# Batch 0's q rows projected from float16 pairs that the load queue transposes

## The chip, the core and the metric

The kernel runs on one core of a Trainium2 chip. A core has five engines with an instruction stream each: TensorE (PE: matrix products and transposes into PSUM; PEld is its weight load), VectorE (DVE), ScalarE (ACT), GpSimd (POOL) and SyncE (SP), on which nearly all DMA transfers of this kernel are issued. The metric is the device time of one execution in microseconds, as the median of several runs. The numbers of the profile come from one profiled execution.

## The reference

Attention with random features over 4 batches and 8 heads (576 rows of 64), then two gated layers. All in float32:

```python
def phi(x):                              # x is q or k, times 64 ** -0.25
    proj = np.einsum('bhsd,md->bhsm', x, omega)        # 128 features
    h = proj - np.sum(x * x, axis=-1, keepdims=True) / 2.0
    h = h - np.max(h, axis=-1, keepdims=True)
    return np.exp(h) / np.sqrt(m)
q_p, k_p = phi(q_s), phi(k_s)
kv  = np.einsum('bhsm,bhsd->bhmd', k_p, v)
num = np.einsum('bhsm,bhmd->bhsd', q_p, kv)
den = np.einsum('bhsm,bhm->bhs', q_p, np.sum(k_p, axis=2))[..., None] + 1e-06
x = (num / den)                          # -> 2304 tokens x 512
h = x @ w_in                             # 512 x 2048
x = (h / (1 + np.exp(-1.702 * h))) @ w_out
out = ((x @ w_a) * (x @ w_b)) @ w_o2     # 512 x 1536, twice; 1536 x 512
```

## The kernel before

**Stages.** Batch 0's attention runs alone, in the first 50 us or so. Then the first gated layer of batch b (`ffn1`) runs interleaved with the attention of batch b+1, token tile by token tile (four of 512 tokens, and one of 256 with the rest rows). The second gated layer (`ffn2`) is last. A product that has to keep float32's accuracy is made of float16 pairs: each operand is a scaled high part (ScalarE) and the remainder, its low part (VectorE), and TensorE makes three products of them.

**Attention, per head pair.** Two heads are worked on together, four head pairs per batch; k of a pair in `kphase32`, q in `qphase`. Both call `features`, which transposes the raw rows (128 partitions of `raw`), projects them on `omega`, takes the maximum of each row (`mx`, line 813), makes the exponent's bias from it and the row's squares `sq` (`mh` and `nb`, line 819) and takes exponentials on ScalarE (`e`, line 779). For batch 0, rows go through TensorE in float32: four transposes against `ident` (line 719), an evacuation with a scale into `xt` (line 665 on VectorE for the names in `EVX`, line 666 on ScalarE for the others), and 16 products that use half of the array's rows each (line 730). For batches 1 to 3 the rows become a float16 pair (`x16`, printed `x_k` or `x_q`; high part at line 734 on ScalarE, low part at line 735 on VectorE), SyncE transposes that by DMA into `xt` (line 740), and TensorE makes two full-array products per block of 128 rows (lines 746 and 747). A head pair's 512 main rows are handled so in batch 0; the remaining 64 rows of all heads go together as `restk` and `restq` (lines 674 to 707). The sum of keys times v is line 874 (and 872 for the rest rows); q's side has transposes of `e` (line 898) and products with it (line 905).

**First gated layer.** `ph` are the three products of h (lines 993 to 995), `th` and `gl` VectorE's part of the gate (lines 1005 and 1015), `gh` ScalarE's, and `y` the three products of the output (1028 to 1030). Line 1029 is the one that uses the low part `gl`.

**Weights.** They come as 64-bit floats, by chunks of 1 MB on SyncE (`wraw`, line 479, two buffers). VectorE turns a chunk into float32 by bit operations (`wf`, lines 493, 533 and 541), ScalarE writes the high part (line 551), VectorE the low part (line 500). Chunks alternate between `w_in` and `w_out`.

**What sets the order.** Each engine's stream is an order written out: the table `ORDER` holds a permutation of the program's instructions for each engine, and an engine executes in that order, so one instruction that waits holds all behind it. SyncE's stream is the load queue too. Its loads are raw rows (line 626; small remainders at 631), rest rows (639), v (`vt` at 650, `vm` at 652) and weights (479). Buffers: the tag A (`x16`, `restk`, `restq`) has two, B (`xt`) two, raw k three, raw q four.

The lines that decide where batch 0 differs:

```python
if nm[1] == "0":                       # batch 0: TensorE transposes
    ...
groups, pairs = (GROUPS_F, PAIRS_F) if nm[1] == "0" else (GROUPS, PAIRS)
```

Of the kernel before, what the change touches and what calls it, by code (L numbers as in the profile page):

```python
# [38 lines left out]
    "uQv0/rnF++cG758fve9twhm+372raBnvOj7uAtwzcu6pOPe8HAtiNSyzNbZQVuku0blrH/eJx1jBe+O7/ifc4z78Xfpz4+Dc4Djh"
    "dveRbzycGxznRsVJy38f+S7kuSt57jKeu47nLuQpB3lvd9fv3JN/7pk/fvl4Zvced2XOXZYzYtQ97u1uaJwbC+cGw2mPItzuMd9A"  # L40
    "OjeSznjQ+5/jP+/j3XA4dw3PXcRzo+LcsDg3Ls4NjHNX9TxdEvfGTze+D3WX79x1PDcwzl35c0PjvFw793Yvt7uPfNf83HU7d+GO"
    "VbvLd+6KxV3yuEsed8nDkt+IOm93u79DfLxdjXdl7tLGjZu4MRMPj3J/euMjjivyPpS1vIscrmSX8l6r9743bsJl7fp2cbuq79JG"
    "eLx7uxsbcYMmXMN3BeOuYHgZcP2ni//e7q5q3FWNu6rx9uX+4D79uE8/7tOPt5eP+1Ce1l2oSC8zHuX+Z/nPe+Mbu3HDJ24gxT2n"
    "cc9p3AWIuxRxVyHuKsRdhbznJe+JzXti8+F799Xk4eXL65YjvUcwHuU+8g2paK949+Fv/MV44buPfIMmxvXhbvfGTy+F98Y3cuJG"
    "TtzIiRs5cSMnbuTEjZy4ERF3aePtHvcw7oLmXdC8C5r3PKfzfGMo71rm8YP7jO4R5HhVvD+9R5D3CPIuY97DyHsY+fRCfJ/5XdW8"
    "pzPv6cx7OvOuQr796z7U03293N7v3RDIu7R5FzTv+qYXda/8XvLveuQ9demV+sZa3ljL45jvTcJR3fuG+96Humc3317HvZDfm3hp"
    "vyc77/Vb90TUw7/88vvI/gp4+U+//N7jRljeCMtyu3v099rP9qfj/h24q18P/7qPclehji+v++UewT3IugdZ9yAr/Cm5d7unru6p"
    "q3s2yjO/L0F5X6Dqnvu6577uua972uue9nr6G3Tv68ncE1tPf5PuQ/lL1f51H+UeafkLdc9B+Xu1f7z8Nl/u870veHlfDvPGaY44"
# [1571 lines left out]
```

## Time and profile before

| | us |
|---|---|
| runs, median of three | 862.88 |
| runs, lowest and highest | 862.5 and 863.72 |
| profiled execution, its own time | 863.73 |
| span of the profiled execution | 861.9 |
| granted TensorE clock, mean | 0.999 of full speed |

The span is the time from the first to the last recorded instruction; the execution takes 1.8 us more. The stages table gives, for a stretch, the time each engine was busy in it and the number of its instructions. The chain of waits goes back from the end: at each moment it names the piece of work that everything behind it stood on. In a timeline an instruction's own time is its record; two records on one engine may overlap by a few hundredths, so what an instruction takes of its engine is better read from one start to the next. Idle time before an instruction stands in brackets, with what ended it.

### The profile page before, as it was taken

The page shows a single profiled execution, that of the slowest core. Times are in us where ns is not written, and L with a number is a line of the kernel's source. Part 1 is how long each engine was busy: PE and PEld are TensorE (multiplying, and loading weights), DVE is VectorE, ACT ScalarE, POOL GpSimd, SP SyncE. Part 2 cuts the span into 40 slices and gives each one's busy share as a digit, 9 for nine tenths or more (in the row PEclk, how much of TensorE's full clock was granted, in tenths as well). Part 3 has the DMA queues.
Part 4 walks back from the last instruction along what each step waited for, and adds up shares of the span by engine and source line. Part 5 has one row for each costly group of instructions (what it writes and reads, how often), then busy time and mean ns, then how long its engine had stood idle before and what let it go on. Part 6 is the DMA issues. An engine that isn't in the chain of part 4 may idle for free.

```text
span 861.9 us, 17314 instructions
## 1 busy us (share of the span) xinstructions
PE 851.8 (99%) x7064; PEld 616.8 (72%) x7064; DVE 677.1 (79%) x1224; ACT 456.6 (53%) x1087; POOL 1.5 (0%) x11
## 2 busy tenths in 40 slices
PE   9999999999999999999999999999999999999997
PEld 7865555455555555444468888889888899888896
DVE  5999999999999977799111489969999758456766
ACT  6997886787767766654232555344543313123221
POOL 0000000000000000000000000000000000000000
PEclk9999999999999999999999999999999999999999
DMA  9977699937674235665110215412522202123312
GB/s 247 245 203 209 177 225 241 222 79 180 146 166 128 77 69 96 140 215 183 49 50 2 83 78 184 159 44 87 183 87 86 44 11 106 68 100 122 89 42 74
DMA packets 138735, 107.71 MB, mean 125 GB/s; under 512 B 107168, under 2 KB 120480, under 8 KB 136608
## 3 DMA queue, kind: packets, MB, share of 16 engines
q1 hardware_dynamic: 138080, 106.05, 45.4%
q8 instruction: 55, 0.90, 0.4%
q10 hardware_dynamic: 576, 0.56, 0.2%
q14 instruction: 24, 0.20, 0.1%
HBM read 71.07 MB, written 17.69 MB: 103 GB/s over the span
## 4 chain that ended last, share of the span: by engine, by line
PE 83%; DVE 9%; DMA 4%; ACT 3%; issue 1%; ACTq 0%; SPq 0%; DVEq 0%
PE ph L993 5%; PE ph L994 5%; PE ph L995 5%; PE y L1029 5%; PE y L1028 5%; PE y L1030 5%; PE paA L1152 3%; PE paA L1153 3%; PE paA L1154 3%; PE pbA L1152 3%; PE pbA L1154 3%; PE pbA L1153 3%; PE oA L1248 3%; PE oA L1250 3%; PE oA L1249 3%; DMA eqT_q<-e_q 2%
## 5 line engine op out<-in xcount | busy, mean ns | idle before, releaser
L1029 PE MATMUL y<-gl,w_out 128*128 128x512 f16 (+1 forms) x320 | 113.6, 358 | 0.3
L1030 PE MATMUL y<-gh,w_out 128*128 128x512 f16 (+1 forms) x320 | 113.3, 358 | 0.0
L1028 PE MATMUL y<-gh,w_out 128*128 128x512 f16 (+1 forms) x320 | 112.0, 358 | 0.0
L1015 DVE SCALAR_TENSOR_TENSOR gl<-th,gh 128x512 f16<-128x512 f32 (+1 forms) x80 | 50.5, 633 | 67.2 <-ACT gh L1014 67.0
L993 PE MATMUL ph<-xT,w_in 128*128 128x512 f16 x256 | 96.9, 379 | 0.6 <-DVE th L1005 0.6
L994 PE MATMUL ph<-xT,w_in 128*128 128x512 f16 x256 | 97.0, 379 | 0.0
L995 PE MATMUL ph<-xT,w_in 128*128 128x512 f16 x256 | 96.8, 379 | 0.0
L1153 PE MATMUL pbA<-forms,w_b 128*128 128x256 f16 (+1 forms) x240 | 61.1, 262 | 0.0
L1152 PE MATMUL pbA<-forms,w_b 128*128 128x256 f16 (+1 forms) x240 | 61.1, 262 | 0.0
L1154 PE MATMUL pbA<-forms,w_b 128*128 128x256 f16 (+1 forms) x240 | 61.0, 262 | 0.0
L1154 PE MATMUL paA<-forms,w_a 128*128 128x256 f16 (+1 forms) x240 | 61.0, 262 | 0.0
L1153 PE MATMUL paA<-forms,w_a 128*128 128x256 f16 (+1 forms) x240 | 61.0, 262 | 0.0
L1152 PE MATMUL paA<-forms,w_a 128*128 128x256 f16 (+1 forms) x240 | 61.0, 262 | 0.0
L1248 PE MATMUL oA<-w_o,ab 128*128 128x256 f16 x216 | 58.9, 273 | 0.3 <-DVE o L1256 0.3
L1250 PE MATMUL oA<-w_o,ab 128*128 128x256 f16 x216 | 58.9, 273 | 0.0
L1249 PE MATMUL oA<-w_o,ab 128*128 128x256 f16 x216 | 58.9, 273 | 0.0
L1162 ACT COPY ka<-paA 128x512 f32<-128x512 f32 (+1 forms) x30 | 16.3, 543 | 77.7 <-PE paA L1154 77.6
L1014 ACT ACTIVATE gh<-th 128x512 f16<-128x512 f32 (+1 forms) x80 | 46.9, 589 | 14.2 <-DVE th L1005 11.5
L1030 PEld LDWEIGHTS <-w_out 128*128 128x128 f16 x320 | 31.2, 98 | 29.4 <-issue 0.8
L995 PEld LDWEIGHTS <-w_in 128*128 128x128 f16 x320 | 31.3, 98 | 28.6
L1162 ACT COPY kb<-pbA 128x512 f32<-128x512 f32 (+1 forms) x30 | 16.3, 542 | 66.7 <-PE pbA L1154 64.2
L994 PEld LDWEIGHTS <-w_in 128*128 128x128 f16 x320 | 31.3, 98 | 27.7 <-issue 0.8
(232 smaller groups left out, 2380.0 us busy)
## 6 DMA issues: line engine op xcount, KB each, us to landing
wraw<-in_moe_w_out_dram SPq DMA_DIRECT2D x14, 1024.0 KB
forms<-fd SPq DMA_DIRECT2D x8, 1792.0 KB
wraw<-in_moe_w_in_dram SPq DMA_DIRECT2D x8, 1024.0 KB
fd<-forms SPq DMA_DIRECT2D x4, 1792.0 KB
wraw<-in_moe_w_a_dram SPq DMA_DIRECT2D x6, 1024.0 KB
wraw<-in_moe_w_b_dram SPq DMA_DIRECT2D x6, 1024.0 KB
rawq<-in_q_dram SPq DMA_DIRECT2D x16, 256.0 KB
vt<-in_v_dram SPq DMA_DIRECT2D x16, 256.0 KB
```

Source lines behind the costliest of these rows:

```text
L993: nc.tensor.matmul(ph[:, :n], w[:, 0, c, fs], xh(c), start=(c == 0), stop=False)
L994: nc.tensor.matmul(ph[:, :n], w[:, 0, c, fs], xl(c), start=False, stop=False)
L995: nc.tensor.matmul(ph[:, :n], w[:, 1, c, fs], xh(c), start=False, stop=(c == KC - 1))
L1028: nc.tensor.matmul(o, w[:, 0, f % 4, cs], gh[f][:, :n], start=(f == 0), stop=False)
L1029: nc.tensor.matmul(o, w[:, 0, f % 4, cs], gl[f][:, :n], start=False, stop=False)
L1030: nc.tensor.matmul(o, w[:, 1, f % 4, cs], gh[f][:, :n], start=False, stop=(f == FC1 - 1))
L1152: nc.tensor.matmul(o[:, i], wh, xh, start=first, stop=False, skip_group_check=True)
L1153: nc.tensor.matmul(o[:, i], wh, xl, start=False, stop=False, skip_group_check=True)
L1154: own["pe"] = nc.tensor.matmul(o[:, i], wl, xh, start=False, stop=final, skip_group_check=True).ins
L1248: nc.tensor.matmul(bank[:, t], lh, wh, start=first, stop=False, skip_group_check=True)
L1249: nc.tensor.matmul(bank[:, t], lh, wl, start=False, stop=False, skip_group_check=True)
L1250: nc.tensor.matmul(bank[:, t], ll, wh, start=False, stop=final, skip_group_check=True)
```

## The change

For q of batch 0 alone (names that begin with `q0`), `features` takes a branch of its own: the 512 main rows become a float16 pair `x16` (ScalarE's high part, VectorE's low part), SyncE transposes it by DMA, and TensorE makes 16 full-array products per head pair, two for each block of 128 rows. k of batch 0 stays as it was, and so do the rest rows. The name `k0_3` is added to `EVX`, so that the evacuation of the last key pair's transposes goes from ScalarE to VectorE. `ORDER` is replaced as a whole, for all engines. Behind the new branch, line numbers are 20 higher.

```diff
 ORDER = (
-    "eNp13b2Oc8myINZXaVy7DWb8kRxPgMYfQICcwRiCrHEkZyBH0LurcgVZ3X3uHePU+bqKZG3ujM0iV0RG/L//9l/+87/9pz/+6+PP"
...
-    VT, FILL, EVX = 4, 10, ('k0_1', 'k0_r')
+    VT, FILL, EVX = 4, 10, ('k0_1', 'k0_3', 'k0_r')
...
     def features(pool, nm, x, e16, e32, psp, extra, shift=0):
 
-        if nm[1] == "0":
+        if nm[:2] == "q0":
+
+            x = x[:, 0 : 2 * NT]
+            x16 = pool.tile([P, 2 * NT, 2, D], F16, tag="A", name=f"x16_{nm}")
+            nc.scalar.activation(out=x16[:, :, 0, :], in_=x, func=AF.Copy, scale=S_QK)
+            nc.vector.scalar_tensor_tensor(
+                out=x16[:, :, 1, :], in0=x, scalar=S_QK, in1=x16[:, :, 0, :],
+                op0=ALU.mult, op1=ALU.subtract,
+            )
+            xt = pool.tile([P, 2 * NT, P], F16, tag="B", name=f"xt_{nm}")
+            own["xt", nm] = nc.sync.dma_start_transpose(
+                out=xt, in_=x16.rearrange("p t j d -> p (t j d)")
+            )
+
+            def project():
+
+                for i in range(2 * NT):
+                    nc.tensor.matmul(pvs[i % 2][:, i // 2, :], xt[:, i, :], om_h, start=True, stop=False)
+                    nc.tensor.matmul(pvs[i % 2][:, i // 2, :], xt[:, i, :], om_l, start=False, stop=True)
+
+        elif nm[1] == "0":
```

What the new table does on SyncE, the load queue, at its head: the difference of the two orders. `rawq` are q's rows, `vt` and `vm` v, `wraw` the first chunk of `w_in`.

```order
-L626 DMA rawq_0_308<-in_q_dram 128x2x256
-L626 DMA rawq_1_357<-in_q_dram 128x2x256
 L650 DMA vt<-in_v_dram 128x8x64 x4
 L652 DMA vm<-in_v_dram 64x4x64 x2
 L479 DMA wraw_157<-in_moe_w_in_dram 128x4x512
-L626 DMA rawq_2_432<-in_q_dram 128x2x256
-L626 DMA rawq_3_489<-in_q_dram 128x2x256
+L626 DMA rawq_0_308<-in_q_dram 128x2x256
+L626 DMA rawq_1_355<-in_q_dram 128x2x256
+L626 DMA rawq_2_436<-in_q_dram 128x2x256
+L626 DMA rawq_3_499<-in_q_dram 128x2x256
```

v and the first chunk of weights now stand ahead of all four loads of q.

Behind that, on SyncE of the changed kernel, come the first chunk of `w_out` (`wraw`), batch 1's first rows, and between them the new transposes (`xt_q` from `x_q`).

```order
 L639 DMA restq<-in_q_dram 64x4x64 x2
 L479 DMA wraw_788<-in_moe_w_out_dram 128x2x1024
 L626 DMA rawk_0_790<-in_k_dram 128x2x256
 L626 DMA rawk_1_793<-in_k_dram 128x2x256
 L631 DMA rawk_1_793<-in_k_dram 128x1x64
 L626 DMA rawq_0_1078<-in_q_dram 128x2x256
 L723 DMA_TRANSPOSE xt_q_0_319<-x_q_0_316 128x8x128
 L631 DMA rawk_0_790<-in_k_dram 128x1x64
 L631 DMA rawq_0_1078<-in_q_dram 128x1x64
 L723 DMA_TRANSPOSE xt_q_1_383<-x_q_1_380 128x8x128
```

The first transpose stands behind `restq`, a chunk of weights and three of batch 1's row loads; the second one follows two small loads later.

On VectorE, around the end of the last key pair (head pair 3), the kernel before:

```order
 L813 TENSOR_REDUCE mx_k_3_1_370<-pa 128x4
 L819 SCALAR_TENSOR_TENSOR mh_k_3_1_371<-mx_k_3_1_370,sq_k_3_271 128x8
 L765 TENSOR_REDUCE sq_q_0_323<-rawq_0_308 128x8
 L819 SCALAR_TENSOR_TENSOR nb_k_3_1_372<-mh_k_3_1_371,sq_k_3_271 128x8
 L493 TENSOR_SCALAR wf_778<-wraw_157 128x1024
 L533 SCALAR_TENSOR_TENSOR wf_778<-wraw_157,wf_778 128x1024
 L683 TENSOR_REDUCE sq_restq<-restq 128x4
```

and the changed kernel, from the first weight instruction on:

```order
 L493 TENSOR_SCALAR wf_802<-wraw_157 128x1024
 L833 TENSOR_REDUCE mx_k_2_1_311<-pa 128x4
 L718 SCALAR_TENSOR_TENSOR x_q_0_316<-rawq_0_308,x_q_0_316 128x8x64
 L839 SCALAR_TENSOR_TENSOR mh_k_2_1_312<-mx_k_2_1_311,sq_k_2_226 128x8
 L839 SCALAR_TENSOR_TENSOR nb_k_2_1_313<-mh_k_2_1_312,sq_k_2_226 128x8
 L833 TENSOR_REDUCE mx_k_3_1_368<-pa 128x4
 L785 TENSOR_REDUCE sq_q_0_321<-rawq_0_308 128x8
```

The first weight instruction and q0's low part now stand ahead of the last key pair's maxima; before, the weight instruction came behind them.

Further down on VectorE of the changed kernel, up to the maxima of q's first head pair:

```order
 L718 SCALAR_TENSOR_TENSOR x_q_1_380<-rawq_1_355,x_q_1_380 128x8x64
 L493 TENSOR_SCALAR wf_809<-wraw_788 128x1024
 L533 SCALAR_TENSOR_TENSOR wf_809<-wraw_788,wf_809 128x1024
 L785 TENSOR_REDUCE sq_q_1_385<-rawq_1_355 128x8
 L541 SCALAR_TENSOR_TENSOR wf_809<-wraw_788,wf_809 128x1024
 L533 SCALAR_TENSOR_TENSOR wf_802<-wraw_157,wf_802 128x1024
 L718 SCALAR_TENSOR_TENSOR x_q_2_452<-rawq_2_436,x_q_2_452 128x8x64
 L833 TENSOR_REDUCE mx_q_0_1_439<-pa 128x4 x2
```

The second chunk (`wf_809`) is converted ahead of the rest of the first one, and the third low part of q stands ahead of q0's maxima.

## Rows read from the trace of the kernel before

**Rows 1.** Stages: us; busy PE, PEld, DVE, ACT, POOL; PEclk; DMA share; GB/s

```profile
0.00:10.00 10.00, 8.58 (x41) 6.28 (x42) 3.94 (x13) 3.71 (x8) 1.53 (x11) 1.00 0.84 227
10.00:20.00 10.00, 9.97 (x96) 8.71 (x95) 6.56 (x17) 8.75 (x28) 0.00 (x0) 1.00 0.98 246
20.00:30.00 10.00, 9.70 (x86) 8.78 (x84) 9.89 (x20) 9.17 (x30) 0.00 (x0) 1.00 0.80 266
60.00:170.00 110.00, 108.60 (x738) 58.75 (x737) 108.72 (x201) 84.94 (x272) 0.00 (x0) 1.00 0.90 214
170.00:300.00 130.00, 129.80 (x983) 68.64 (x980) 123.31 (x275) 97.06 (x242) 0.00 (x0) 1.00 0.56 134
```

**Rows 2.** Chain of waits, 0 to 200 us: start, us, what decided

```profile
16.15 1.73 PE pa L874 x16
...
25.92 0.43 ACT w_in L551
...
47.99 0.60 DVE wf L493
...
98.58 0.60 DVE gl L1015
...
136.16 7.96 DMA eqT_q<-e_q
...
191.59 3.58 DMA xt_q<-x_q
```

**Rows 3.** Timeline of VectorE and TensorE: start, us, engine, line, operation, tiles, idle before

```profile
63.27 1.29 DVE L1015 SCALAR_TENSOR_TENSOR gl<-th,gh 128x512 f16<-128x512 f32 x2
...
64.06 0.38 PE L1029 MATMUL y<-gl,w_out 128*128 128x512 f16 x1
...
234.34 0.69 DVE L1015 SCALAR_TENSOR_TENSOR gl<-th,gh 128x512 f16<-128x512 f32 x1
...
235.16 0.38 PE L1029 MATMUL y<-gl,w_out 128*128 128x512 f16 x1
...
261.88 0.69 DVE L1015 SCALAR_TENSOR_TENSOR gl<-th,gh 128x512 f16<-128x512 f32 x1 [0.17 <-ACT gh L1014]
...
264.13 0.38 PE L1029 MATMUL y<-gl,w_out 128*128 128x512 f16 x1
```

**Rows 4.** Timeline of VectorE, first 32 us

```profile
6.12 0.69 DVE L765 TENSOR_REDUCE sq_k<-rawk 128x8 f32<-128x512 f32 x1 [1.19 <-ACT rawk L763]
...
9.34 0.68 DVE L665 TENSOR_SCALAR xt_k<-pa 128x512 f32<-128x512 f32 x1
...
12.28 0.76 DVE L691 TENSOR_REDUCE mx_restk<-pa 128x2 f32<-128x256 f32 x2 [1.33 <-PE pa L688]
...
19.12 1.29 DVE L813 TENSOR_REDUCE mx_k<-pa 128x4 f32<-128x512 f32 x2 [1.73 <-PE pa L730]
...
22.10 0.69 DVE L493 TENSOR_SCALAR wf<-wraw 128x1024 int32<-128x1024 int32 x1
...
28.00 0.69 DVE L813 TENSOR_REDUCE mx_q<-pa 128x4 f32<-128x512 f32 x1
...
31.16 0.75 DVE L735 SCALAR_TENSOR_TENSOR x_k<-rawk,x_k 128x576 f16<-128x576 f32 x1
...
31.82 1.22 DVE L500 SCALAR_TENSOR_TENSOR w_in<-wf,w_in 128x1024 f16<-128x1024 f32 x1
```

**Rows 5.** Timeline of TensorE: transposes and projections of q, float16 projections of k

```profile
15.27 0.66 PE L719 MATMUL pa<-ident,rawq 128*128 128x128 f32 x4
...
26.55 2.01 PE L730 MATMUL pa<-om_f,xt_q 64*128 64x128 f32 x16
...
39.82 1.16 PE L730 MATMUL pa<-om_f,xt_q 64*128 64x128 f32 x16
...
50.46 0.22 PE L746 MATMUL pa<-om_h,xt_k 128*128 128x128 f16 x1
...
50.52 0.22 PE L747 MATMUL pa<-om_l,xt_k 128*128 128x128 f16 x1
```

More of the change, by code (lines that the diff above doesn't have):

```diff
@@ L39 @@
[L39 to L48, printed above, removed]
@@ L304 @@
[L304 to L307 removed]
+    "eNp13b1uc1mzIOZbaZz4C7jqj6QzA558AANOBhMYjiaxk4ETw/duradIvd3HZ4JW65W4KXKv2pT4VK2q/+ff/vN/+rf/6a//8vjX"
@@ new lines @@
+    "X+dff8W//sp//VX/+qv/9df866/nv/56/euv98+37rd/vnB+vnJ+vnR+vhY/X4t7zM9B8XNU/BwWP8fFz23i5/t5v/dzTPzcPu/x"
+    "P/8+P7c9P7c9P7c9P7fNn3/X/e/n33l/8s/t697+/vvn87y3+bm//jm+f47vn9v2z+3y3ubnZ9TP1+vn63WP/blt/dy2fr4+P/+e"
+    "+xx+/j0//37eY+/T+vla/9xv3/v8uY++t/25j/n5/vzc9/zcZn6+Pz/fe/58/XX/+/n66+frr3tCfj5//tz36+f2r/v/n/t73bP0"
+    "c/vX/Tk/t3v/HPP++f775/vve/uf2zzvsT+3e977/bnd+97u5+vvn6+/f77+vqfZeb4n6nHP1OOeqntezz2x557Zc0/nuef33JN6"
+    "Hve7j/vdx/3a497kcW/y8N17f3ehzl2pE07/vVOLaRUsgzW1qFbIEt21ORb8ruSxfHc9T1rAe+xdonPX59yFOneVzl2Wc9fl3EU9"
@@ new lines @@
+    "ZaXvsXeNzl3kc1fp3CU+5Xb32LtqcU953LWKe+Ljrljc0x33fMc9sfEUXfeIGw/nBsS5EXFuSJwWU25yH4sPd43PXeRzV/fcsDh3"
+    "fc+4yb2Xp3txp/drI9Lv124snBtE5z60cx/auQ/o3Ad07gM69wEdD+gu9Lkrft7+eZ/RXcu4axl3jcLy3AA4Lzf2w++d3iA7N6LO"
+    "DalzY+3cwDo34s4Nr3Pj6dygOTdqztsl6Bq8Z0gcvNzz/dpxYd6fe3z3XoMPD+ie4oeb3HN6Vz/uSsdd6bhxEDcOwtXtcnY9u4hd"
+    "1S75vebvPbvq0+Xvs3vEjYi4ERE3IuJGRNyIiBsHceMgbmxEecXwM+5NbpjFDbPwsnGjJG5shNi48RI3XuIufNwFjbtQMV5j7v3d"
+    "pY0bEXEjIm5ExF2KsBTttene6V3paF+7d/r24b5a3dXKu1p5z2nec5p33fLh9csL2r3JPbF5T2zek5j3JKaTeOMlxmf3Z9wIi7vc"
@@ new lines @@
+    "cRc57iLHXeR0Jm8IxF3uuMsdd7nj5cXSd+9h1vJGSdzVjxthcSMsvaB6hb0hlXd9865v3nXLexIz/aD7WfjsPtxw7H244ZXXybk/"
+    "/IZU3hDI417u3d/Hly+vtPeIu3h5lyzvouR9uPny2T3i5Yj7w+/Dzftw8z7c8pLutdwDv2uZNwTyhkDeFcy7gnlXMP0OuAufdy3r"
+    "nue657mc57v6eVc/2xH3n/f6zXv95g3CvD8t70+r+8zrPvPyzP0W8evkxmT65eG3h+d24yX9Umn/vDduv3vujW+UZLvx/f2SPtzf"
+    "Uveu6t5V7V35zXW/ds9G3bNR92zUPRvlbDgH9xUk7ytI3XNf99yX32J+je3vwvtdZ2N8uDe5YVbHZ/eh+R15wyxvmOV9gaq7eHV8"
+    "dn/4/Vrfh9v34bbfoulr7/u70Km7d//0K/be1X3FzBuxeSM2b8Tmjdga93cfuMd8lycFzb3A8l5g+fYL2W/k+2TudVT3Oqq7PPX0"
@@ L308 @@
+    "pfZC/00I9Pkt/H1+sxH9y/vxm5zYmt/zW/N7vnmOLUfuf1QTeyHyKvXva4jPl+23HPnX7r0gecXZOuD+Jg62VPhPpW980w+bAHl9"
+    "sxteL7ZU+JtH2Feb529mZGt5/1my6wXANe+l5t8VCP8zcfApC35/UgP7srEFuI/fetz86P++eFjF928KwOpuRfD5reqdf6YK/lkg"
+    "rAr3/Jbn/ruq3k0J/o8Kejdf8O8Ldf/r//v/AWJT5CI="
 )
```

512 lines of the change are left out of this document (252 added, 260 removed).

## The prediction, made before the changed kernel ran

> **What bounds the kernel now.** I read the busy time by stage first, then the chain of waits, then the timelines of VectorE and TensorE where the change lies. By stage [rows 1], TensorE's matmul time is near the whole of every stretch after 10 us (9.97 and 9.70 of 10, then 108.60 of 110 and 129.80 of 130), at a granted clock of 1.00 throughout, which is the level of 2.4 GHz. VectorE is busy 3.94 and 6.56 of 10 us in the first two stretches, then 9.89 of 10, 108.72 of 110, and 123.31 of 130. So VectorE has no room from 20 to 170 us, and it has room before: 6.06 us up to 10, 3.44 us up to 20.
>
> The chain [rows 2] says when each engine decides. In the first 48 us it runs on TensorE and ScalarE (a key product at 16.15, a weight copy at 25.92). At 47.99 it goes over to VectorE, with the conversion of weights, and stays there, with short stretches of issue between, until the low part of a gate at 98.58. Behind that it is mostly TensorE, with transposing transfers in it: 7.96 us at 136.16, 3.58 us at 191.59.
>
> That TensorE looks full behind 100 us doesn't free VectorE from the account. The low parts of the gate that VectorE starts at 63.27 (two in a row) are first used by TensorE at 64.06, and the one that starts at 234.34 and takes 0.69 us is used at 235.16, 0.13 us after its end [rows 3]. Each such pair makes TensorE late if VectorE is late. These two are the first and the last of ten pairs that are less than 0.3 us apart; behind them leads are longer, as the 1.56 us from the end of the one of 261.88 to its use at 264.13. So what VectorE loses up to 235 us is handed to TensorE, which has no idle time to win it back; a loss of a microsecond or so later is not.
>
> **The change part by part.** *Added on VectorE.* Each of the four head pairs of batch 0's q gets one low part. The same instruction for a later batch, 576 wide, starts at 31.16 and the next at 31.82, 0.66 us apart for 0.75 us of record; 512 wide that scales to 0.59, and I take 0.60 [rows 4]. Four are 2.4 us. The name k0_3 puts one more evacuation on VectorE; one that is there has 0.68 us of record (9.34), less the same overlap of 0.09, so 0.60 again. Sum: 3.0 us more work, all of it ahead of the first gates that bound TensorE. Nothing on VectorE is removed, since q's evacuations were ScalarE's.
>
> *Removed from TensorE.* For each head pair four f32 transposes go (0.66 us) and 16 half-array f32 products (2.01 us at 26.55, 1.16 us at 39.82) [rows 5]. Added are 16 float16 products; two that follow each other start at 50.46 and 50.52, so 0.06 us each, 1.0 us. A pair saves 0.8 to 1.7 us, four save 3.3 to 6.7. ScalarE trades an evacuation for a high part of the same width, and gives one evacuation (k0_3) away: about 0.6 us less work.
>
> *How long that saving counts.* TensorE ends the chain only up to 48 us; from there VectorE does. So TensorE's saving is worth something as far as it lets VectorE start its early work earlier. VectorE's early idle time is 1.19 us at 6.12, 1.33 us at 12.28 and 1.73 us at 19.12, each ended by TensorE or by ScalarE's squares [rows 4]: 4.25 us, the three largest pieces. Between 0 (none filled) and 4.25 lies what the change can recover.
>
> *The order on VectorE.* I walked down the new order with the durations above, starting each instruction at the later of its predecessor's end and its data; 20.1 and the waits below are what it gives, estimates from these rows. The key maxima of the last head pair no longer have q's transposes and products in front of them, and the first weight instruction (0.60) stands among them. VectorE comes to the end of the last key pair's small instructions at about 20.1, where before it came there at 22.10 (the weight row that followed) [rows 4]. By then it has done 1.8 us more: the weight instruction, q0's low part, the evacuation. That is 2.0 + 1.8 = 3.8 us recovered. I take 3.8, the value of the walk; the bound above is 4.25.
>
> *The load queue.* Early transfers run at 227, 246 and 266 GB/s in the three stretches [rows 1], so 2.27, 4.73 and 7.39 MB are over at 10, 20 and 30 us. Ahead of the first weight chunk now stand omega, k, restk and v, 2.4 MB; with the chunk's 1.05 MB it lands at 10 + (3.45 - 2.27) / 0.246 = 14.8 us. q0 (0.26 MB) follows at 15.9, and q1 to q3 by 19.1; q0 was used at 15.27 before [rows 5], so it is late by half a microsecond against that, but its first reader now is ScalarE. restq ends at 19.6, w_out's first chunk at 23.9, and batch 1's first rows, which stand ahead of the first transpose, at about 26.6. The first transposed q then lands at 28 to 30 us, against the maximum of that q at 28.00 before [rows 4].
>
> *New waits.* The walk gives three on VectorE. The squares of restq wait for their load: 0.5 us. The next conversion waits for w_out's chunk, which stands behind all of q: 0.8 us. The third low part waits for a buffer of tag A, of which there are two, so for the first transpose to be over: about 1 us. Behind that low part on VectorE are q0's maxima and the whole conversion; TensorE and ScalarE wait for them. None of the three is in the trace, so each could be 0 if the transfer lands early; together they lie between 0 and the price of the nearest transposes in the chain, 3.58 us [rows 2]. I take 2.0, near the middle, by the walk. Other q transposes behind the first wait in the same queue, but they have the conversions to cover them.
>
> *Sum.* 3.0 - 3.8 + 2.0 = **+1.2 us**. The profiled execution took 863.73 with a span of 861.9; this gives a span of 863.1 and 864.9 us for that execution. It lies 0.85 us above the median of the runs, 862.88, and against the median the forecast is **864.1 us**, 862.6 to 865.6 with 1.5 us for the terms of the walk. That is within 0.2% (1.7 us), about what a measurement of this kernel can tell from no change.
>
> **The rivals.** *TensorE's saving counts (faster).* The chain's first 48 us lie on TensorE and ScalarE [rows 2], and TensorE's weight loads fill 8.71 and 8.78 of 10 us from 10 to 30 against 58.75 of 110 later [rows 1]. So the array is really full early, where the change takes work off it. If VectorE's new waits don't appear and half of the 5.0 us in the middle of the saving comes through (the other half meets ScalarE's pieces of the chain), it is 862.9 - 2.5 = 860.4. Against it: VectorE is full from 20 us on. The Trainium skill, page "Perfetto Trace Analysis", section "Identifying the Most-Contended Engine", says to judge TensorE by its weight-load time and not by its matmul time, which leads to this rival; the rows agree with it for the early stretches and show matmul time near 100% where weight loads are near a half.
>
> *The added VectorE work is not covered (slower).* If the key chain ahead of it keeps VectorE waiting as before, for v and the chunk in front of q delay nothing that it waits for and hasten nothing, the last key pair's small instructions end at 22 us or later, and 3.0 us go straight into the gates: 865.9. It decides where VectorE reaches that point later than about 21.9 in the changed kernel. This is also the case in which the moved loads do nothing for the time.
>
> *The transposes are late (slower).* They stand behind w_out's chunk and batch 1's rows in one queue, and a transfer that takes 3.58 to 7.96 us is in the chain twice [rows 2], where TensorE's own four transposes took 0.66 [rows 5]. If the first lands at 32 instead of 28 to 30, VectorE stands at q0's maxima and everything behind them: +4 us, 866.9. It decides from a landing at about 31 us. The Trainium skill, page "VectorE: DVE Perf Modes", section "The three transpose paths", gives 390 ns for TensorE and 1309 ns for the DMA's transposing path for 128x128, and its rules prefer TensorE where the result may go to PSUM; this speaks for the rival, and the rows agree in the order of the two, with four on TensorE in 0.66 us.
>
> **How the numbers follow.** The forecast has 0.47, the faster rival 0.25, uncovered VectorE work 0.16, late transposes 0.12. The forecast's own range lies mostly within 0.2%: of its 0.47, 0.34 is there, 0.10 above 864.6 and 0.03 below 861.2. So faster 0.25 + 0.03 = 0.28, same 0.34, slower 0.10 + 0.16 + 0.12 = 0.38. The range takes in the rivals' times with some 0.5 us beyond: 859.9 to 867.3.
>
> **What would show it.** Right: VectorE at the last key pair's small instructions near 20 us, its idle time in the first 20 us down by about 2 us or more, the first q transpose landing at 28 to 30, a wait of about 1 us at the third low part, and the gate of 234.34 later by about 1 us. The saving counts if that gate is earlier by 2 us or more. Uncovered work shows as that gate 3 us later with no waits at 20 to 40 us. Late transposes show as VectorE idle ahead of q0's maxima, put down to a transfer. Wrong altogether would be a change that begins after 235 us, where VectorE has a lead, or another granted clock.

## The result: slower by one per cent

| | before | changed |
|---|---|---|
| median, us | 862.88 | 871.54 |
| lowest and highest of three | 862.5 and 863.72 | 871.12 and 872.62 |
| profiled execution, its span, us | 861.9 | 870.8 |
| granted clock, mean over the span | 0.999 | 0.992 |
| ratio, 95% interval | | 1.0099 [1.0085, 1.0113] |

Five more runs of the changed kernel, beside the last experiment, have a median of 872.73, ratio 1.0098 [1.0076, 1.0120]. The time is 8.7 us over the kernel before and above the range that was given. Six executions (one more of the changed kernel, two of a2_more_idle and three of a3_transposes_first below, 882.07 to 884.22) lie some 10 us above the other runs of their kernels and are left out of medians; the two of them that were profiled have TensorE's products twice as long up to 42 us and more, and their traces are not used for the change.

The stages of the changed kernel, in the columns of [rows 1]: the stretch's length, busy time of TensorE, its weight loads, VectorE, ScalarE and GpSimd, the granted clock, the DMA engines' share, GB/s.

```profile
0.00:10.00 10.00, 8.36 (x56) 6.08 (x58) 5.27 (x15) 4.70 (x12) 1.53 (x11) 1.00 0.90 216
10.00:20.00 10.00, 9.68 (x78) 8.62 (x74) 8.68 (x21) 7.92 (x27) 0.00 (x0) 1.00 1.08 314
20.00:30.00 10.00, 8.91 (x46) 8.39 (x46) 7.81 (x14) 6.34 (x23) 0.00 (x0) 0.58 0.88 206
30.00:40.00 10.00, 8.98 (x68) 7.86 (x67) 5.68 (x12) 6.88 (x19) 0.00 (x0) 0.74 0.50 107
60.00:170.00 110.00, 106.75 (x733) 58.65 (x732) 108.60 (x204) 83.50 (x277) 0.00 (x0) 1.00 0.82 210
170.00:300.00 130.00, 128.51 (x956) 67.60 (x954) 122.89 (x273) 96.58 (x235) 0.00 (x0) 1.00 0.60 138
```

The third column from the end has the surprise: the granted clock, 1.00 in every stretch of [rows 1], is 0.58 and 0.74 of full speed between 20 and 40 us. In the same stretches VectorE is busy 7.81 and 5.68 of 10 us. From 60 us on little is different: TensorE has 1.9 and 1.3 us less work in the two long stretches. In steps of one microsecond, where the clock falls and where it comes back:

```profile
20.00:21.00 1.00, 0.57 (x4) 0.47 (x4) 0.92 (x3) 0.32 (x2) 0.00 (x0) 1.00 0.97 379
21.00:22.00 1.00, 0.70 (x9) 0.69 (x8) 0.40 (x1) 1.00 (x4) 0.00 (x0) 0.81 1.08 366
22.00:23.00 1.00, 1.00 (x8) 0.78 (x5) 0.67 (x3) 1.00 (x4) 0.00 (x0) 0.50 1.11 339
...
35.00:36.00 1.00, 1.00 (x16) 1.00 (x16) 0.46 (x3) 0.51 (x2) 0.00 (x0) 0.87 0.02 5
```

0.50 is the lower of the two levels, 1.2 GHz. TensorE goes down to it between 21 and 22 us and up again between 35 and 36 us, so 13.6 us are spent at the lower level (13 of them whole, and the parts that 0.81 and 0.87 stand for). Its own timeline there (start, us, engine, line, operation, tiles, count; idle time before it in brackets):

```profile
14.08 1.90 PE L894 MATMUL pa<-vt,e_k 128*128 128x65 f32 x16
...
20.43 0.41 PE L674 MATMUL pa<-ident,restq 128*128 128x128 f32 x2 [0.57 <-DMA restq<-in_q_dram]
...
21.31 0.99 PE L688 MATMUL pa<-om_f,xt_restq 64*128 64x128 f32 x8 [0.30 <-ACT xt_restq L666]
...
24.96 3.52 PE L894 MATMUL pa<-vt,e_k 128*128 128x65 f32 x16
...
31.46 0.31 PE L730 MATMUL pa<-om_h,xt_q 128*128 128x128 f16 x1
31.57 0.31 PE L731 MATMUL pa<-om_l,xt_q 128*128 128x128 f16 x1
...
35.29 0.22 PE L730 MATMUL pa<-om_h,xt_q 128*128 128x128 f16 x1
35.35 0.22 PE L731 MATMUL pa<-om_l,xt_q 128*128 128x128 f16 x1
```

The same sixteen products of keys and v take 1.90 us at 14.08 and 3.52 us at 24.96. The float16 products of q, which the change brought in, start 0.11 us apart at 31.46 and 0.06 us apart at 35.29. Just ahead of the fall stand two short waits, 0.57 us for the rows of `restq` and 0.30 us for ScalarE. VectorE's timeline shows what that does to it:

```profile
20.82 0.17 DVE L839 SCALAR_TENSOR_TENSOR nb_k<-mh_k,sq_k 128x8 f32<-128x8 f32 x1
...
21.60 0.42 DVE L683 TENSOR_REDUCE sq_restq<-restq 128x4 f32<-128x256 f32 x1 [0.61 <-ACT restq L681]
...
24.02 0.69 DVE L493 TENSOR_SCALAR wf<-wraw 128x1024 int32<-128x1024 int32 x1
...
27.04 0.69 DVE L785 TENSOR_REDUCE sq_q<-rawq 128x8 f32<-128x512 f32 x1 [1.08 <-ACT rawq L783]
...
30.89 0.69 DVE L718 SCALAR_TENSOR_TENSOR x_q<-rawq,x_q 128x512 f16<-128x512 f32 x1 [0.89 <-ACT x_q L717]
...
33.83 1.29 DVE L833 TENSOR_REDUCE mx_q<-pa 128x4 f32<-128x512 f32 x2 [2.25 <-PE pa L731]
...
36.32 0.69 DVE L785 TENSOR_REDUCE sq_q<-rawq 128x8 f32<-128x512 f32 x1 [0.80 <-ACT rawq L783]
```

At 20.99 the last key pair's small instructions are done, 0.9 us behind the forecast and 1.2 ahead of the kernel before. Behind that VectorE waits again and again, the longest time (2.25 us) for TensorE's projection of q, whose maxima come at 33.83 instead of 28.00 [rows 4]. The gate that answers to the second pair of [rows 3]:

```profile
241.13 0.69 DVE L1035 SCALAR_TENSOR_TENSOR gl<-th,gh 128x512 f16<-128x512 f32 x1
...
242.17 0.38 PE L1049 MATMUL y<-gl,w_out 128*128 128x512 f16 x1
```

It is 6.8 us later, and its use 7.0. The first gate starts 8.1 us later than before (the window up to its end is 72.04 us instead of 63.95), the span is 8.9 us longer. So nearly all of the loss is there at the first gate, as the argument of [rows 3] said a loss on VectorE would be.

One more thing sets the two profiles apart. The first sixteen products of keys, in the kernel before, in the changed kernel, and in two versions that come below, c1_clock_held and c3_low_twice:

```profile
5.62 2.67 PE L730 MATMUL pa<-om_f,xt_k 64*128 64x128 f32 x16
```

```profile
5.61 1.49 PE L750 MATMUL pa<-om_f,xt_k 64*128 64x128 f32 x16
```

```profile
5.86 1.49 PE L750 MATMUL pa<-om_f,xt_k 64*128 64x128 f32 x16
```

```profile
6.03 2.67 PE L751 MATMUL pa<-om_f,xt_k 64*128 64x128 f32 x16
```

The same group takes 2.67 us or 1.49 us, though the granted clock reads 1.00 there each time. In the executions with 2.67 us TensorE comes up to its full level only at about 10 us, in the others before 5.6 us. It differs between c1 and c3, which do the same up to there, so it belongs to the execution and not to the change. The profile of the kernel before is of the late kind (as are a1, b1, b2, b3 and b4 below), that of the changed kernel of the early kind (as are a3, a4, c1, c2, c4 and e1).

### The profile page after: what moved, and what is told of

Its sections match the earlier page's. It is cut to its first block, busy times and chain, and to the rows that moved or that the text cites. A ratio compares the mean times of both kernels' runs of the same rounds, so it can differ in the third digit from the quotient of the medians.

```text
span 870.8 us, 17290 instructions
## 1 busy us (share of the span) xinstructions
PE 852.7 (98%) x7048; PEld 618.8 (71%) x7048; DVE 681.6 (78%) x1229; ACT 457.9 (53%) x1086; POOL 1.5 (0%) x11
## 4 chain that ended last, share of the span: by engine, by line
PE 82%; DVE 10%; DMA 4%; ACT 2%; issue 1%; SPq 0%; ACTq 0%; DVEq 0%
PE y L1048 6%; PE y L1050 6%; PE y L1049 6%; PE ph L1013 5%; PE ph L1014 5%; PE ph L1015 5%; PE paA L1172 3%; PE oA L1268 3%; PE paA L1174 3%; PE pbA L1172 3%; PE pbA L1173 3%; PE pbA L1174 3%; PE oA L1270 3%; PE paA L1173 3%; PE oA L1269 3%; DMA eqT_q<-e_q 2%
```

## The experiments

Four causes were weighed: the granted clock; the moved loads, by themselves; the idle products (the order table also moves eight of the products named `idle`, which compute nothing that is used, from the start to 37.65 us); VectorE's added work. The expectations are quoted as written. Unless it says otherwise the diff is against the kernel named in the heading's line. Lines of loads and products in the diffs are those of the order, shortened. Shifts are starts in the profiled execution against the same instruction in the kernel before.

### The moved loads alone, at either clock: a1_moved_loads, b4_moved_loads_idle

Against the kernel before, SyncE's order only:

```diff
-L626 DMA rawq_0, rawq_1
 L650 DMA vt x4
 L652 DMA vm x2
 L479 DMA wraw (w_in, first chunk)
+L626 DMA rawq_0, rawq_1
```

> The kernel before, with one part of the change alone: in the load queue v and the first weight chunk stand ahead of q0 and q1. Theory M (the moved loads are the loss): about 870 us, near the changed kernel's 871.5. Theory C (the loss is the clock that falls in the changed kernel at about 21.8 us and stays at its lower level until 35) and theory Q (the loss is the path of q through the transposing transfers): q0 comes at about 16 us and TensorE wanted it at 15.27, so up to 1 us, 862.5 to 864.5, with the granted clock at 1.00 from 20 to 40 us.

b4 adds 18 idle products to a1, ahead of the four transposes of q's first head pair:

```diff
-    VT, FILL, EVX = 4, 10, ('k0_1', 'k0_r')
+    VT, FILL, EVX = 4, 28, ('k0_1', 'k0_r')
...
+L1466 MATMUL idle<-om_h 128x256 x18
 L719 MATMUL pa<-ident,rawq_0 x4
```

> The kernel before with v and the first weight chunk ahead of q0 and q1 in the load queue, which took 874.2 us with a wait of 1.92 us on TensorE for q0 and the clock at its lower level behind it, now with 18 idle products (nobody reads them) in that wait. Theory G: the clock stays up, and the wait alone remains: 863.5 to 866. If the moved loads cost something else too, 868 or more.

a1: 874.19 (four runs, 873.18 to 875.98), ratio 1.0113 [1.0062, 1.0165]. b4: 866.30 (ten runs), ratio 1.0045 [1.0027, 1.0063]. Stages and TensorE of a1, then of b4:

```profile
10.00:20.00 10.00, 8.08 (x66) 7.34 (x65) 5.42 (x14) 7.29 (x24) 0.00 (x0) 0.83 1.05 270
20.00:30.00 10.00, 10.00 (x52) 9.20 (x52) 4.89 (x10) 3.58 (x13) 0.00 (x0) 0.50 0.50 179
...
16.74 1.08 PE L719 MATMUL pa<-ident,rawq 128*128 128x128 f32 x4 [1.92 <-DMA rawq<-in_q_dram]
...
18.05 3.51 PE L874 MATMUL pa<-vt,e_k 128*128 128x65 f32 x16
```

```profile
20.00:30.00 10.00, 9.92 (x93) 9.13 (x89) 9.14 (x18) 8.69 (x29) 0.00 (x0) 1.00 0.75 246
...
15.08 2.14 PE L1466 MATMUL idle<-om_h 128*128 128x256 f16 x18
...
17.71 1.90 PE L874 MATMUL pa<-vt,e_k 128*128 128x65 f32 x16
```

In a1 TensorE waits 1.92 us for q's rows and goes on at half the clock: busy 10.00 of 10 us from 20 to 30, and VectorE 4.89. In b4 the same loads come in the same order, idle products stand where the wait was, and the clock stays. The medians differ by 7.9 us, 7.5 if each is taken against the kernel before that ran beside it (863.63 and 863.28). One of b4's ten runs has a mean clock of 0.990, and took 873.67; of the nineteen runs of the kernel before beside a1, two have 0.987 and 0.990, and took 872.0 and 871.17 where the median is 863.63. Where in those three runs the clock was low is not on record. So a fall of the clock is worth 7 to 8 us in this kernel, with nothing else changed but idle products; in a1 the lower level holds for some 20 us, longer than the 13.6 us of the changed kernel. Without it, moved loads and idle products together cost 3.0 us (866.30 against 863.28).

### Idle products where the changed kernel waits: a2_more_idle, b1_idle_back, b3_idle_back_more

a2 is the changed kernel with ten idle products more, six ahead of the transposes of `restq` and four ahead of its projections:

```diff
-    VT, FILL, EVX = 4, 10, ('k0_1', 'k0_3', 'k0_r')
+    VT, FILL, EVX = 4, 20, ('k0_1', 'k0_3', 'k0_r')
...
+L1486 MATMUL idle<-om_h 128x256 x6
 L674 MATMUL pa<-ident,restq x2
...
+L1486 MATMUL idle<-om_h 128x256 x4
 L688 MATMUL pa<-om_f,xt_restq x8
```

> The changed kernel with ten more idle products on TensorE (nobody reads them): six ahead of restq's transposes, where TensorE waited 0.57 us at 20.43, four ahead of restq's projections, where it waited 0.30 us at 21.31. Theory C: the granted clock stays at 1.00 from 20 to 40 us, the 16 products with v that took 3.52 us at 24.96 take about 1.9, and of the 8.7 us some 5 to 7 go, as the lower level held for 13 us: 864.5 to 867. Theory Q: the transposes bring q as late as before, 869 to 871.5, with the clock up or not.

b1 moves eight idle products of the changed kernel back to where they were:

```diff
 L750 MATMUL pa<-om_f,xt_k_0 x8
+L1486 MATMUL idle<-om_h 128x256 x8
...
 L731 MATMUL pa<-om_l,xt_q_1
-L1486 MATMUL idle<-om_h 128x256 x8
```

> The changed kernel with eight idle products of TensorE (nobody reads them) put back where the kernel before has them: its order has 13 in a row from about 9.1 us, the changed one only five at 7.03 and nine at 37.65. Theory I (the moved idle products are the loss: the clock no longer holds through the first 40 us): the granted clock stays at 1.00, 864 to 867, eight of them costing up to 0.9 us of TensorE. Theory G (the clock falls for TensorE's waits behind the moved loads): it falls near 21 us all the same, 871 to 873.

b3 has both edits:

```diff
-    VT, FILL, EVX = 4, 10, ('k0_1', 'k0_3', 'k0_r')
+    VT, FILL, EVX = 4, 20, ('k0_1', 'k0_3', 'k0_r')
...
+L1486 MATMUL idle<-om_h 128x256 (b1's eight, a2's six and four)
```

> The changed kernel with the eight idle products put back early and ten more (nobody reads them) around restq's transposes and projections, where TensorE waited 0.57 and 0.30 us. Theories I and G alike: the clock stays at 1.00 from 10 us on, and what is left above the kernel before is the changed path itself: 864 to 867. If it stays at 870 or above with the clock up, the path of q is the loss (theory Q).

| | median | ratio, 95% interval |
|---|---|---|
| a2_more_idle, eight runs | 868.84 | 1.0049 [1.0015, 1.0083] |
| b1_idle_back, four runs | 872.37 | 1.0107 [1.0091, 1.0122] |
| b3_idle_back_more, four runs | 872.69 | 1.0137 [1.0091, 1.0183] |

a2 is 5.2 us over the kernel before beside it, where the changed kernel is 8.7 over, so it gains some 3.5 us; no trace of these runs shows its clock. b1 and b3 gain nothing. Stages of b1 where its clock falls:

```profile
33.00:36.00 3.00, 1.14 (x8) 0.73 (x9) 2.83 (x7) 3.00 (x11) 0.00 (x0) 1.00 1.14 148
36.00:39.00 3.00, 2.44 (x25) 2.10 (x25) 2.96 (x5) 2.99 (x10) 0.00 (x0) 0.84 1.02 219
39.00:42.00 3.00, 3.00 (x20) 3.00 (x20) 2.42 (x7) 2.40 (x6) 0.00 (x0) 0.50 0.87 164
```

The fall at 21 us is gone from b1, and there is one at 38 us instead: from 33 to 36 us TensorE has had work for 1.14 of 3 us, while VectorE (2.83) and ScalarE (3.00) are full. b3 loses the clock at about 37 us too. The time is that of the changed kernel, though b1's lower level lasts only about 7 us there; b1 and b3 also have the late start, which the changed kernel's profile has not.

### The loads in another order: a3_transposes_first, a4_restq_first

a3 is the changed kernel with the third and fourth transposes of q ahead of batch 1's v on SyncE, a4 has the rest rows of q ahead of q:

```diff
 L723 DMA_TRANSPOSE xt_q_1
+L723 DMA_TRANSPOSE xt_q_2, xt_q_3
 L626 DMA rawq_1 (batch 1)
 L652 DMA vm (batch 1)
 L650 DMA vt x2 (batch 1)
-L723 DMA_TRANSPOSE xt_q_2, xt_q_3
```

> The changed kernel with one difference in the load queue: the third and fourth transpose of q stand ahead of batch 1's v, whose loads wait for TensorE's last reads of v until 34.68 us. Theory Q: the third transpose is issued at about 32 us instead of 35.14, VectorE and ScalarE come to q2 earlier, and 2 to 3 us are won: 868.5 to 869.5. Theory C: the clock is as in the changed kernel, the stretch from 22 to 35 us stays as slow, and what is won is under 1 us: 870.5 to 871.5.

```diff
 L479 DMA wraw (w_in, first chunk)
+L639 DMA restq x2
 L626 DMA rawq_0, rawq_1, rawq_2, rawq_3
-L639 DMA restq x2
```

> The changed kernel with restq ahead of q0 in the load queue, behind the first weight chunk. restq landed at 20.3 us and should land at about 16. Theory C, if it is TensorE's 0.57 us of waiting for that load that lets the clock fall: the wait is gone, the clock stays at 1.00 from 20 to 40 us, and the time is 864.5 to 867. If the clock falls for the waits behind it all the same, or by theory Q: 870 to 872, since q0 to q3 come half a microsecond later.

a3: 874.02 (seven runs), ratio 1.0106 [1.0076, 1.0136]. The third transpose is issued at 33.99 instead of 35.14 us, and the clock is 0.59 and 0.72 in the two stretches from 20 to 40 us: no gain, so these transposes aren't what is waited for. a4: 875.34 (four runs), ratio 1.0114 [1.0068, 1.0160]. Its stages:

```profile
19.00:20.00 1.00, 0.89 (x6) 0.75 (x6) 0.96 (x5) 1.00 (x5) 0.00 (x0) 0.77 1.02 391
20.00:21.00 1.00, 1.00 (x7) 1.00 (x6) 0.59 (x1) 0.90 (x4) 0.00 (x0) 0.50 1.03 410
```

The wait for `restq` is gone, and the clock falls all the same, earlier even. So it isn't that one wait either. It fits b1 and b3: where one wait is closed the clock falls at another. That this is because TensorE has less work in the new order and stands behind more work of others is argued from the rows, not shown by a run of its own.

### The idle products as a cause: b2_idle_away

The kernel before, with the eight idle products moved away as the change does:

```diff
 L674 MATMUL pa<-ident,restk x2
-L1466 MATMUL idle<-om_h 128x256 x8
...
 L730 MATMUL pa<-om_f,xt_q_0 x8
+L1466 MATMUL idle<-om_h 128x256 x8
```

> The kernel before with eight of its 13 early idle products moved to its other two, at about 28.5 us; nothing else is different. Theory I: the clock falls or rises late, 870 to 876. Theory G: the clock stays at 1.00, 862 to 864.5.

862.97 (ten runs), ratio 1.0002 [0.9992, 1.0012]. Moving them costs nothing where TensorE has its other work, and moving them back in the changed kernel (b1) gives nothing. This cause falls.

### The changed kernel with the clock held: c1_clock_held, c1_again

28 idle products counted instead of 10: eight more behind the early five, six and four around `restq` as in a2, and the late ones kept:

```diff
-    VT, FILL, EVX = 4, 10, ('k0_1', 'k0_3', 'k0_r')
+    VT, FILL, EVX = 4, 28, ('k0_1', 'k0_3', 'k0_r')
...
+L1486 MATMUL idle<-om_h 128x256 (x8 early, x6 ahead of L674 restq, x4 ahead of L688)
```

> The changed kernel with its ten idle products of TensorE where it has them and 18 more (nobody reads them): eight behind its early five, six and four around restq's transposes and projections. Theory C (the loss is mostly the clock, which falls because TensorE waits more): the granted clock stays at 1.00, 865 to 867, so 4.5 to 6.5 of the 8.7 us are the clock and the rest is the changed path at full clock. If the clock stays up and it is still 870 or more, the clock is not the cause.

869.65 (seven runs, 868.48 to 877.58), ratio 1.0084 [1.0053, 1.0114]; the profiled execution, 868.48, has a span of 866.7. The same kernel once more, as c1_again, with this expectation:

> The same kernel as c1_clock_held, for the comparison with d1 to d3 on one chip: 868 to 870.

869.71 (ten runs), ratio 1.0068 [1.0045, 1.0091], span 867.6. Stages and TensorE of c1_clock_held:

```profile
20.00:30.00 10.00, 9.40 (x91) 8.54 (x90) 9.09 (x17) 9.14 (x29) 0.00 (x0) 1.00 0.94 229
30.00:40.00 10.00, 8.42 (x90) 7.34 (x90) 9.71 (x22) 9.29 (x27) 0.00 (x0) 1.00 0.98 193
...
24.28 1.90 PE L894 MATMUL pa<-vt,e_k 128*128 128x65 f32 x16
```

At full clock VectorE is busy 9.09 and 9.71 of 10 us again. The span comes down by 4.1 us (870.8 to 866.7; 3.2 to c1_again's), with the early start in all three profiles. Against the kernel before of the same set of runs, the changed kernel is 8.7 and 9.8 us over by its two medians, c1 6.3 and 6.4, so 2.2 to 3.5 us less. The intervals of the ratios overlap, so the medians alone would not settle it; the spans and a2 agree with them. The clock is thus, as an estimate, between a quarter and a half of the loss, and 4.8 or 5.7 us by the spans, 6.4 by the medians, are left without it. Since the kernel before was profiled with the late start and c1 with the early one, what the spans leave may be too little.

### What is left at full clock: c2_q_first, c3_low_twice, c4_more_vector, e1_no_low

All but c4 are c1_clock_held with an edit. c2 puts the first two loads of q ahead of v and the weight chunk again:

```diff
+L626 DMA rawq_0, rawq_1
 L650 DMA vt x4
 L652 DMA vm x2
 L479 DMA wraw (w_in, first chunk)
-L626 DMA rawq_0, rawq_1
```

> The kernel of c1_clock_held with q0 and q1 ahead of v and the first weight chunk in the load queue again, as before. Theory L (at full clock the moved loads are what is left, as they cost 3 us alone in the kernel before with its clock held up): 862.5 to 864.5, some 2 to 3 us under c1. Theory P (VectorE's 3.0 us of new work is what is left): within 1 us of c1.

871.36 (five runs), ratio 1.0088 [1.0054, 1.0121]; the span is 866.7, as c1's. Taking the moved loads back gains nothing, so they are not what is left.

c3 computes each low part of q twice, 2.4 us more for VectorE:

```diff
+            for _ in range(2):
-            nc.vector.scalar_tensor_tensor(
+                nc.vector.scalar_tensor_tensor(
```

> The kernel of c1_clock_held with each of q's four low parts computed twice on VectorE, 4 x 0.6 = 2.4 us more of its work at the place of the low parts. Theory P (VectorE's work there is not covered): 2 to 2.5 us over c1. If that work is covered by waits: under 1 us over c1.

871.91 (six runs, 869.67 to 876.74), ratio 1.0098 [1.0069, 1.0128], 2.3 us over c1 by the medians, with intervals that overlap; span 870.0, 3.3 us over c1, with the first gate 4.1 us later. But c3's profile has the late start and c1's the early one, so these two differences are not the low parts' alone.

e1 goes the other way and takes the low parts from VectorE: the low half is filled with zeros by GpSimd in their place (at 11.85, 22.31, 26.87 and 29.47 us), so that q's products use the high parts alone.

```diff
-            nc.vector.scalar_tensor_tensor(
-                out=x16[:, :, 1, :], in0=x, scalar=S_QK, in1=x16[:, :, 0, :],
-                op0=ALU.mult, op1=ALU.subtract,
-            )
+            nc.gpsimd.memset(x16[:, :, 1, :], 0.0)
```

> The kernel of c1_clock_held without q's four low parts: GpSimd writes zeros in their place ahead of time, so the low part of q is left out of the products. Theory P (VectorE's new work is what is left at full clock): 2.4 us less on VectorE, the first gate's low part 2 us or more earlier than in c1's profile (67.15), the time 2 to 3 us under c1's 868.5 to 869.7: 866 to 867.5. Theory Q (the path through the transposes is what is left): q comes 0.6 us earlier, and the time is at most 1 us under c1.

869.13 (six runs), ratio 1.0083 [1.0052, 1.0113], span 865.1. Stages up to the end of the first gate, of the kernel before (with 20 to 40 us apart), of c1, and of e1 from 20 us on:

```profile
0.00:20.00 20.00, 18.54 (x135) 14.99 (x136) 10.49 (x28) 12.46 (x34) 1.53 (x11) 1.00 0.91 237
20.00:40.00 20.00, 19.36 (x170) 17.51 (x170) 19.89 (x42) 18.64 (x55) 0.00 (x0) 1.00 0.92 266
20.00:63.95 43.95, 42.22 (x341) 33.93 (x340) 43.58 (x96) 40.54 (x134) 0.00 (x0) 1.00 0.85 227
```

```profile
0.00:20.00 20.00, 18.14 (x135) 15.00 (x136) 13.25 (x34) 12.05 (x35) 1.54 (x11) 1.00 0.97 251
20.00:67.15 47.15, 42.29 (x351) 33.02 (x350) 45.75 (x93) 40.52 (x129) 0.00 (x0) 1.00 0.89 228
```

```profile
20.00:66.75 46.75, 41.90 (x346) 32.64 (x346) 43.68 (x90) 39.94 (x127) 1.67 (x4) 1.00 0.92 227
```

Before, VectorE has 10.49 + 43.58 = 54.07 us of work up to 63.95. In c1 it is 13.25 + 45.75 = 59.00 us up to 67.15: 4.9 us more work and 1.7 us less idle time, so the gate is 3.2 us later; how much of the lower idle time is c1's early start is not shown. In e1 (with the early start, as c1) work behind 20 us falls by 45.75 - 43.68 = 2.1 us and idle time rises from 1.40 to 3.07: the gate is only 0.4 us earlier.

The same stretches of c3:

```profile
0.00:20.00 20.00, 18.53 (x120) 14.94 (x121) 11.36 (x29) 10.12 (x28) 1.52 (x11) 1.00 0.94 256
20.00:71.26 51.26, 44.29 (x365) 34.79 (x364) 50.32 (x102) 43.01 (x135) 0.00 (x0) 1.00 0.80 208
```

In c3 VectorE has 2.7 us more work than c1 up to the gate, and 1.4 us more idle time; the idle time grows in the first 20 us (8.64 against 6.75 us), where the late start lies, and not behind them (0.94 against 1.40). So the added work is paid in about full there, where VectorE has hardly any idle time to give. Less work brings a fifth (e1): VectorE then waits 1.0 us for projections of q and 0.9 us for ScalarE's squares of q, and in c1 for neither. So VectorE's low parts may be part of what is left, but taking them away alone gives back 0.1 to 0.2 us by the medians (6.2 over the kernel before against 6.3 and 6.4) and 1.6 or 2.5 us by the spans (865.1 against 866.7 and 867.6), less than the runs of one kernel differ among themselves.

c4 asks the same of the kernel before, with five sums of squares computed twice, about 3 us more for VectorE and nothing else changed:

```diff
-            nc.vector.tensor_reduce(out=sq[:, 0:TB], in_=x, axis=AX.X, op=ALU.add)
+            for _ in range(2 if nm[:2] == "q0" or nm == "k0_3" else 1):
+                nc.vector.tensor_reduce(out=sq[:, 0:TB], in_=x, axis=AX.X, op=ALU.add)
```

> The kernel before with five reductions of squares on VectorE done twice (q0 to q3 and the last key pair), 5 x 0.6 = 3.0 us more of its work, all else the same. Theory P: 865.5 to 867 at a granted clock of 1.00, the 3.0 us in full. If VectorE's early idle time takes half of it: 864 to 865. If TensorE waits so long that the clock falls: over 869.

867.09 (twelve runs, 864.55 to 876.19), ratio 1.0055 [1.0029, 1.0082]. A stretch of the profiled execution, 870.78, and the wait of TensorE in it:

```profile
40.00:50.00 10.00, 8.44 (x61) 8.05 (x60) 9.16 (x26) 7.43 (x24) 0.00 (x0) 0.75 0.79 205
...
43.12 1.11 PE L906 MATMUL pa<-kv,eT_q 128*128 128x65 f32 x8 [1.56 <-ACT e_q L780]
```

With nothing but VectorE's extra work TensorE waits 1.56 us for an exponential, and the clock falls behind that. The seven runs of c4 with a mean clock of 0.997 or more took 864.55 to 867.57, with a median of 865.30, 2.0 us over the 863.34 of the kernel before beside them: about two thirds of VectorE's 3 us come out. The three with 0.992 or less took 871.77 to 876.19, 8.4 to 12.9 us over it.

### VectorE's work given to others: d1_low_on_pool, d2_evac_back, d3_both

d1 is c1_clock_held with the low parts on GpSimd, d2 with the evacuation of `k0_3` on ScalarE again, d3 has both:

```diff
-            nc.vector.scalar_tensor_tensor(
-                out=x16[:, :, 1, :], in0=x, scalar=S_QK, in1=x16[:, :, 0, :],
-                op0=ALU.mult, op1=ALU.subtract,
-            )
+            nc.gpsimd.tensor_scalar(out=xs, in0=x, scalar1=S_QK, scalar2=None, op0=ALU.mult)
+            nc.gpsimd.tensor_tensor(out=x16[:, :, 1, :], in0=xs, in1=x16[:, :, 0, :], op=ALU.subtract)
```

> The kernel of c1_clock_held with q's four low parts computed on GpSimd (a scaled copy, then a subtraction) instead of VectorE. Theory P (VectorE's new work is what is left at full clock): 2.4 us less on VectorE, the first gate's low part some 2 us earlier than in c1, the time 1.5 to 2.5 us under it, 866 to 867.5. Theory Q (q's late arrival through the transposes is what is left): GpSimd is slower, q comes later still, and the time is that of c1 or more.

```diff
-    VT, FILL, EVX = 4, 28, ('k0_1', 'k0_3', 'k0_r')
+    VT, FILL, EVX = 4, 28, ('k0_1', 'k0_r')
```

> The kernel of c1_clock_held with the name k0_3 taken out of EVX again: the evacuation of the last key pair's transposes is ScalarE's, behind that of the pair ahead of it. Theory P: 0.3 to 0.6 us under c1. Theory Q: the same as c1, or later by up to 0.6 if ScalarE is the busier one there.

```diff
-    VT, FILL, EVX = 4, 28, ('k0_1', 'k0_3', 'k0_r')
+    VT, FILL, EVX = 4, 28, ('k0_1', 'k0_r')
...
+            nc.gpsimd.tensor_scalar(out=xs, in0=x, scalar1=S_QK, scalar2=None, op0=ALU.mult)
+            nc.gpsimd.tensor_tensor(out=x16[:, :, 1, :], in0=xs, in1=x16[:, :, 0, :], op=ALU.subtract)
```

> d1_low_on_pool and d2_evac_back together: none of the 3.0 us of new work is on VectorE. Theory P: the first gate's low part within 1 us of the kernel before, the time 2 to 3 us under c1, 865.5 to 867. Theory Q: as c1 or above.

| six runs each | median | ratio, 95% interval |
|---|---|---|
| d1_low_on_pool | 872.57 | 1.0087 [1.0056, 1.0117] |
| d2_evac_back | 874.23 | 1.0114 [1.0072, 1.0157] |
| d3_both | 874.51 | 1.0135 [1.0091, 1.0178] |

None gains, and none answers what it was made for, since the clock came down in the early stretches of all three profiles (0.91 in d1 from 20 to 30 us, for one). In d1 GpSimd takes 1.82 us for a scale and 1.16 us for a subtraction where VectorE took 0.69 for both:

```profile
16.85 1.82 POOL L719 TENSOR_SCALAR xs_q<-rawq 128x512 f32<-128x512 f32 x1 [14.74 <-DVE sq_k L784]
18.75 1.16 POOL L720 TENSOR_TENSOR x_q<-xs_q,x_q 128x512 f16<-128x512 f32 x1
```

The changed kernel as it is was run beside e1 to give the second median above, under the label after_again:

> The changed kernel once more, beside the same runs of before: 871 to 873 with the granted clock at its lower level from about 22 to 35 us in the profiled run.

No version was faster than the kernel before.

## Why the prediction was wrong, step by step

- **What bounds the kernel.** Borne out: a loss ahead of the first gates is handed on nearly whole. +8.1 us at the first gate, +6.8 at the gate of [rows 3], +8.9 at the end.
- **Added work on VectorE, 3.0 us.** The instructions are there with the durations taken (low parts of 0.69 us, the second evacuation). But the account stopped short: up to the first gate VectorE has 4.9 us more in c1. The new table also puts a fourth low part of batch 1's keys ahead of that gate (four at L755, three at L735 before, 0.75 us each), which the walk down the order had not counted.
- **Early idle time recovered, 3.8 us.** The number came out, with luck. VectorE's busy time in the first 20 us goes from 10.49 to 13.95 us in the changed kernel, 3.46 more, and the last key pair's small instructions end at 20.99, forecast 20.1, where before VectorE came there at 22.10. But the rows that the walk started from are of an execution with the late start, and the changed kernel's profile has the early one. Where the new order started late, the same point comes at 23.49 (b3), 24.03 (b1) and 24.30 (c3), later than in the kernel before, and VectorE's busy time in the first 20 us is 11.60, 11.12 and 11.36 us, so only 0.6 to 1.1 us are recovered. These three have at least eight more idle products ahead of that point, which take about 0.9 us at the full level, so not all of the difference is the start. How much of the 3.46 us is the order's is open.
- **New waits on VectorE, 2.0 us.** This is the term that failed. The three places were found: 0.61 us at the squares of `restq` (forecast 0.5), none at the chunk of `w_out` (0.8), 0.89 at the third low part (about 1, though ended by ScalarE's high part and not by a transpose). The sum is not: from 20 to 40 us VectorE's idle time is 0.11 us before (busy 19.89 of 20, in the rows under e1) and 6.51 us in the changed kernel (20 less the 7.81 and 5.68 above), 6.4 us more. The rest of them, 2.25 us at q's maxima and 1.08 and 0.80 at squares, stand in or just behind the stretch in which TensorE runs at half its clock; in c1, with the clock up, there are 1.20 us of idle time instead of 6.51.
- **The clock taken as given.** That is the step behind it. The prediction read 1.00 in every stretch of [rows 1] and kept it for the changed kernel; it named another clock at its end as what would make it wrong, and gave that no chance. The rows that spoke for it were there: TensorE's 9.97 and 9.70 of 10 us from 10 to 30 [rows 1] held work that the change takes away (the four transposes at 15.27 and the sixteen products of 2.01 us at 26.55 [rows 5]), and the change puts work of VectorE, ScalarE and the load queue ahead of what TensorE has left. The clock was not 1.00 throughout before, either: up to about 10 us that profile ran at the lower level, as the 2.67 us of its first sixteen products show. a1 and b4 show the price of a fall, and c1 what the sum comes to with the clock held: up to 40 us, 3.0 - 2.76 (13.25 against 10.49 in the first 20 us) + 1.09 (20 less 9.09 and 9.71, against 0.11) = +1.3, where +1.2 was forecast. That the two agree is in part luck, since the 2.76 us are of an execution with the early start. Up to the first gate c1 loses another 1.9 us.
- **The load queue.** The rest rows of q landed at 20.3 us, worked out as 19.6, and w_out's chunk came in time. Moving the loads costs nothing at full clock in c2; in the kernel before, they and 18 idle products cost 3.0 us together (b4). The transposes were not waited for by TensorE up to 40 us; a3 shows that hastening the last two gives nothing.
- **The rivals.** The saving on TensorE came out as a loss: the float16 products are as short as worked out, 0.06 us apart at the full clock, but TensorE then stood waiting, and its clock fell. Uncovered VectorE work was on the right side, with the right mechanism for a part (c4), but it priced 3.0 us where 8.7 were lost; its condition, VectorE at the last key pair's small instructions later than 21.9, did not hold in the changed kernel's profile and holds in b1, b3 and c3. Late transposes fall: the 2.25 us ahead of q0's maxima end with TensorE and not with a transfer.

What stays open: of the 4.8 to 6.4 us that are left at full clock, 3.2 us stand at the first gate in c1's profile, where VectorE has 4.9 us more work; the rest is added in small pieces up to the end of the span (+3.9 us by the 28th gate, +4.7 by the 64th), and no experiment singled out a cause. c1 itself carries 18 idle products more, whose own cost in it was not measured. And which start each run of a median had is not on record, so how much of the difference between medians is the start stays open too.
